# One landmark-attention and two-layer gated-MLP kernel: V of the second head group loaded ahead of the weights, landmark sums moved from VectorE to GpSimd

## The chip, the cores and the metric

The kernel runs on one core of a Trainium2 chip. The metric is device microseconds (us) of one execution. Before the change the median of three runs is 918.29 us (917.45 to 919.88).

## The reference, cut to what matters

Inputs: q, k, v of shape (4, 8, 576, 64): 4 batches, 8 heads, 576 tokens, head size 64; two gated layers with weights of 512 x 1536 (gate and value) and 1536 x 512 (out).

```python
q_lm = q.reshape(B, H, 32, 18, D).mean(axis=3)      # landmarks: means of 18 neighbouring tokens
k_lm = k.reshape(B, H, 32, 18, D).mean(axis=3)
A  = softmax(scale * q    @ k_lm.T)                 # 576 x 32
Bm = softmax(scale * q_lm @ k_lm.T)                 # 32 x 32
C  = softmax(scale * q_lm @ k.T)                    # 32 x 576
Z  = Bm.T / (norm1(Bm) * norminf(Bm) + 1e-6)
for _ in range(6): Z = 2 * Z - Z @ Bm @ Z           # an iterated inverse
attn = A @ Z @ C @ v                                # heads side by side: x of 2304 x 512
x = (silu(x @ w_gate) * (x @ w_val)) @ w_out
y = (sigmoid(x @ w2_gate) * (x @ w2_val)) @ w2_out
```

The landmark sums of q and k (18 tokens at a time) and the loading of v are what the change touches.

## The kernel before, in words

The eight heads of a batch are worked in two groups of four, so that four heads times 32 landmarks fill 128 partitions. One unit of attention work is (b, g): batch b, head group g; AORDER lists the eight units in order. q and k of a unit are loaded as 128 partitions (head, landmark) x 18 tokens x 64; v as 96 partitions.

`front(b, g)` does one unit. Its inner `lm_steps` runs first for k and then for q: the 18 tokens are summed to a tile `lm` of 64 elements (L121, VectorE), ScalarE copies it beside itself (L122), TensorE transposes it (L125, tile `lt`), ScalarE evicts it with a mask (L128, tiles `bdk`, `bdq`), and nine transposes (L135, `tp`) with three ScalarE copies (L136) lay out the tokens themselves in `kq`. Then come the scores of C (`cs`, L157 takes their maximum, L162 the exponential `e`), those of Bm (`bm`, `bs`), the transposes of e (`et`, `eT`), the product with v (`cv`, 48 matmuls), whose eviction L193 writes the second half of tile `bc`, and the scores of A (`as`, `sx`).

`back(b)` needs both units of a batch. L238 to L258 normalise Bm and work out the scale `rr`, a chain of small VectorE instructions; L273 to L284 are the six products of the iteration (`nw` on TensorE, 16 small matmuls, then `rw` on VectorE, each waiting for the other). The first `nw` reads `bc`, so it waits for `cv` of both groups. Iteration carries Z @ C @ v along, so its result `ut` is all that the first layer needs.

The first layer works on chunks c of 256 columns of d_ff: `uw_steps` (U) multiplies ut by the chunk's weights, `gv1_steps` (G) makes gate and value, `o1_steps` (O) the output. Weights are 32-bit words that two ScalarE and two VectorE instructions convert (L314, L317, L319, L323), out weights with one more each (L350, L351). They arrive in three `raw` buffers, so a load waits until ScalarE has read the buffer's former content.

The order is written out by hand as a list of words: `I0+F00 F01 B0+F10 U00 F11 J0 B1 G00 I1 F20 ...`, where F is a front, B a back, I and J finish weights, and "+" interleaves two. The framework's planner takes that order as priority and orders each engine's queue by what its own cost model says is ready; the engines then run their queues strictly in that order. All loads are issued by SyncE's queue, in order. Tiles of one tag share a fixed number of buffers: `in` (q and k) has 4, `vin` (v) 1, `lm` 2, `rw` 3, `wo` (out weights of a chunk, 8 KB a partition) 2.

Before the loop, k, q, v of unit (0,0) and k, q of (0,1) are loaded; v of (0,1) is asked for by `load_next` at the end of `cv` of (0,0), since `vin` has one buffer.

Of the kernel before, what the change touches and what calls it, by code (L numbers as in the profile page):

```python
# [5 lines left out]
F32 = mybir.dt.float32  # L6
# [3 lines left out]
ALU = mybir.AluOpType  # L10
AX = mybir.AxisListType
# [3 lines left out]
def nystrom_moe_kernel(tc, q, k, v, wg1, wv1, wo1, wg2, wv2, wo2, out):  # L15
    nc = tc.nc
    B, H, S, D = q.shape
    M = 32
    P = 128
    L = S // M  # L20
    R = 6
    TP = S // R
    HS = S // 2
    DM = H * D
# [7 lines left out]
    def pool(name, side=None, **kw):  # L32
        return tc.alloc_tile_pool(name=name, bufs=1, side=side, reuse_waits="tile", **kw)

    cst = pool("cst")
    per = pool("per")
    att = pool("att")
# [23 lines left out]
    def mm(o, l, r, start=True, stop=True):  # L61
        nc.tensor.matmul(o, l, r, start=start, stop=stop, skip_group_check=True)  # L62
# [3 lines left out]
    inq = {}  # L66

    def load_attn(b, which, g):
        if which == "v":
            t = att.tile([TP, 4, R, D], F32, tag="vin", name=f"vin{b}_{g}", bufs=1)  # L70
            nc.sync.dma_start(t, v[b, 4 * g:4 * g + 4].rearrange("h (p r) d -> p h r d", r=R))
        else:
            t = att.tile([P, L, D], F32, tag="in", name=f"{which}in{b}_{g}", bufs=4)
            src = {"q": q, "k": k}[which]
            nc.sync.dma_start(t, src[b, 4 * g:4 * g + 4].rearrange("h (t u) d -> (h t) u d", u=L))
        inq[which, b, g] = t

    NU = L // 2

    AORDER = [(b, g) for b in range(B) for g in range(2)]  # L80

    def flat(x):
        return x.rearrange("p a b -> p (a b)")

    def load_next(b, g, which):
        i = AORDER.index((b, g)) + (1 if which == "v" else 2)
        if i < len(AORDER):
            load_attn(AORDER[i][0], which, AORDER[i][1])

    def step(fill, n=1):  # L90
        while n and fill:
            try:
                next(fill[0])
                n -= 1
            except StopIteration:
                fill.pop(0)
# [4 lines left out]
    def small(tag, shape, nm_, bufs=2):  # L101
        return att.tile(shape, F32, tag=tag, name=f"{tag}{nm_}", bufs=bufs)

    def pst(b, shape, nm, g=0):

        tag = "n" if nm in ("nw", "ut") else "a"
        if b == 0:
            tag = {"tp": "gv", "cs": "o", "as": "o"}.get(nm, tag)
        return ptile(shape, tag, f"{nm}_{b}_{g}")

    def front(b, g):
# [3 lines left out]
        def sm(tag, shape, bufs=2):  # L115
            return small(tag, shape, nm_, bufs)

        def lm_steps(which):
            src = inq[which, b, g]
            lm = sm("lm", [P, 2, D])  # L120
            nc.vector.tensor_reduce(lm[:, 0], src.rearrange("p u d -> p d u"), axis=AX.X, op=ALU.add)  # L121
            nc.scalar.copy(lm[:, 1], lm[:, 0])  # L122
            yield
            ps = pst(b, [P, P], "lt", g)
            nc.tensor.transpose(ps, flat(lm), ident)  # L125
            bdt = sm("bd" + which, [P, 2, P], 1)
            for w in range(2):
                nc.scalar.activation(bdt[:, w], ps, AF.Copy, scale=pmask[:, w:w + 1])  # L128
            yield
            t = sm("kq", [P, NU, P])  # L130
            for i in range(3):
                ps = pst(b, [P, 3, P], "tp", g)
                for j in range(3):
                    u = 3 * i + j
                    nc.tensor.transpose(ps[:, j], flat(src[:, 2 * u:2 * u + 2]), ident)  # L135
                nc.scalar.copy(t[:, 3 * i:3 * i + 3], ps)  # L136
                yield
            load_next(b, g, which)
            return bdt, t
# [41 lines left out]
        for hf in range(2):  # L181
            ps = pst(b, [TP, 3, P], "et", g)
            for j in range(3):
                r = 3 * hf + j
# [14 lines left out]
        for i0, i1 in ((0, 5), (5, NU)):  # L199
            ps = pst(b, [P, 5, 2 * M], "as", g)  # L200
            for i in range(i0, i1):
                for h in range(4):
                    hs = slice(M * h, M * h + M)
                    mm(ps[hs, i - i0].rearrange("p (w m) -> p w m", w=2), qT[:, i, hs], bdk[:, :, hs])
            x = flat(ps[:, 0:i1 - i0]).rearrange("p (u m) -> p u m", m=M)
# [3 lines left out]
                                    op=ALU.subtract)  # L209
# [21 lines left out]
    def back(b):  # L231

        def sm(tag, shape, bufs=2):
            return small(tag, shape, b, bufs)

        bs, bsm, BC = BS[b]

        nc.vector.tensor_scalar(bsm, bsm, 1e-9, None, op0=ALU.add)  # L238
        nc.vector.reciprocal(bsm, bsm)
        nc.vector.tensor_tensor(bs, bs, bsm[:, :, None].to_broadcast([P, 2, M]), op=ALU.mult)  # L240
        nc.scalar.copy(BC[:, :, 0:M], bs)

        bmt = sm("bmt", [P, 2, M])
        nc.vector.transpose(out=flat(bmt), in_=flat(bs))
        nrm = sm("nrm", [P, 2, 2])
        nc.vector.tensor_reduce(nrm[:, 0], bs, axis=AX.X, op=ALU.add)
        nc.vector.tensor_reduce(nrm[:, 1], bmt, axis=AX.X, op=ALU.add)
        yield
        nb = sm("nb", [P, 4, M], 1)
        nc.vector.tensor_copy(nb, nrm.rearrange("p a b -> p (a b)")[:, :, None].to_broadcast([P, 4, M]))  # L250
        nbt = sm("nbt", [P, 4, M], 1)
        nc.vector.transpose(out=flat(nbt), in_=flat(nb))
        nmax = sm("nmax", [P, 2, 2])
        nc.vector.tensor_reduce(flat(nmax), nbt, axis=AX.X, op=ALU.max)
        rr = sm("rr", [P, 2])
        nc.vector.tensor_tensor(rr, nmax[:, 0], nmax[:, 1], op=ALU.mult)
        nc.vector.tensor_scalar(rr, rr, 1e-6, None, op0=ALU.add)
        nc.vector.reciprocal(rr, rr)  # L258
        yield


        def prod(x):
            ps = pst(b, [P, 2, 96], "nw")
            for g in range(2):
                for h in range(4):
                    hs = slice(M * h, M * h + M)
                    mm(ps[hs, g], x[hs, g, 0:M], x[hs, g])
            return ps

        ga = [a_steps(b, g) for g in range(2)]  # L270
        ps = prod(BC)
        RW = sm("rw", [P, 2, 96], 3)
        nc.vector.tensor_tensor(RW, ps, rr[:, :, None].to_broadcast([P, 2, 96]), op=ALU.mult)  # L273
        yield
        for it in range(5):
            ps = prod(RW)
            RW2 = sm("rw", [P, 2, 96], 3)
            nc.vector.scalar_tensor_tensor(RW2, RW, 2.0, ps, op0=ALU.mult, op1=ALU.subtract)
            RW = RW2
            step(ga)  # L280
            yield
        ps = prod(RW)
        UU = flat(sm("rw", [P, 2, 96], 3))[:, 0:P].rearrange("p (g d) -> p g d", g=2)
        nc.vector.scalar_tensor_tensor(UU, RW[:, :, M:], 2.0, ps[:, :, M:], op0=ALU.mult, op1=ALU.subtract)  # L284
        yield
        ps = pst(b, [P, P], "ut")
        nc.tensor.transpose(ps, flat(UU), ident)
        nc.vector.tensor_copy(flat(UT[b]), ps)
        yield
        while ga:  # L290
            step(ga)
            yield

    for g in range(2):
        for x in "kqv" if g == 0 else "kq":
            load_attn(0, x, g)


# [359 lines left out]
```

## Time and profile before

| what | value |
|---|---|
| median of three runs | 918.29 us |
| profiled execution | 917.74 us, of which the span from the first to the last instruction is 915.9 us |
| TensorE (PE) busy | 877.8 us, 96% |
| VectorE (DVE) busy | 542.2 us, 59% |
| ScalarE (ACT) busy | 391.7 us, 43% |
| GpSimd (POOL) busy | 0.7 us |

How to read the rows below. [...] A row of the timeline gives start, duration, engine, line, operation, the tiles written and read and how many instructions are merged; brackets at its end give how long the engine was idle before and what released it. A row of the groups by line gives busy us and mean ns behind the bar. A row for one tile gives durations in ns (minimum, median, maximum), then the first and last start. PE is TensorE's matmul, SPq is SyncE's queue, which issues the loads. All times are us from the start of the span.

### The profile page before, as it was taken

The page shows a single profiled execution, that of the slowest core. Times are in us where ns is not written, and L with a number is a line of the kernel's source. Part 1 is how long each engine was busy: PE and PEld are TensorE (multiplying, and loading weights), DVE is VectorE, ACT ScalarE, POOL GpSimd, SP SyncE. Part 2 cuts the span into 40 slices and gives each one's busy share as a digit, 9 for nine tenths or more (in the row PEclk, how much of TensorE's full clock was granted, in tenths as well). Part 3 has the DMA queues.
Part 4 walks back from the last instruction along what each step waited for, and adds up shares of the span by engine and source line. Part 5 has one row for each costly group of instructions (what it writes and reads, how often), then busy time and mean ns, then how long its engine had stood idle before and what let it go on. Part 6 is the DMA issues. An engine that isn't in the chain of part 4 may idle for free.

```text
span 915.9 us, 16047 instructions
## 1 busy us (share of the span) xinstructions
PE 877.8 (96%) x6588; PEld 741.9 (81%) x6588; DVE 542.2 (59%) x1093; ACT 391.7 (43%) x853; POOL 0.7 (0%) x6
## 2 busy tenths in 40 slices
PE   5499899999999999999999999999999999999997
PEld 4356877778898998998998888888888888888886
DVE  6988857746968678769961154346238236323343
ACT  5568568545725446428652263134116114111111
POOL 0000000000000000000000000000000000000000
PEclk9599999999999999999999999999999999999999
DMA  7666211003513113203110022003004000000132
GB/s 230 222 209 182 70 53 49 7 1 93 155 31 93 47 47 116 69 1 95 46 44 4 0 71 68 1 28 110 0 1 138 1 1 24 1 0 1 47 93 69
DMA packets 27081, 57.66 MB, mean 63 GB/s; under 512 B 4224, under 2 KB 7296, under 8 KB 27008
## 3 DMA queue, kind: packets, MB, share of 16 engines
q1 hardware_dynamic: 25280, 54.28, 19.6%
q10 hardware_dynamic: 1728, 2.36, 1.1%
q8 instruction: 51, 0.84, 0.4%
q14 instruction: 22, 0.18, 0.1%
HBM read 51.90 MB, written 4.72 MB: 62 GB/s over the span
## 4 chain that ended last, share of the span: by engine, by line
PE 88%; DVE 5%; ACT 4%; DMA 1%; issue 1%; SPq 0%; ACTq 0%
PE po L62 33%; PE pg L62 24%; PE pv L62 23%; PE pu L62 3%; PE tp L135 2%; PE nw L62 1%; DMA qin<-in_q_dram 1%; DVE lm L121 1%; PE cs L62 1%; ACT e L162 1%; PE as L62 1%; DVE hl L351 0%; ACT L162 0%; PE et L185 0%; DVE h L441 0%
## 5 line engine op out<-in xcount | busy, mean ns | idle before, releaser
L62 PE MATMUL po<-hh,wo 128*128 128x288 f32 x768 | 162.1, 302 | 1.1 <-DVE uw L351 0.7
L512 DVE TENSOR_TENSOR hf<-hf,pv 128x512 f32<-128x512 f32 (+1 forms) x60 | 38.0, 634 | 193.0 <-PE pv L62 193.0
L62 PE MATMUL po<-wo,h 128*128 128x512 f32 x648 | 152.2, 390 | 0.0
L62 PEld LDWEIGHTS po<-wo,h 128*128 128x128 f32 x648 | 121.1, 188 | 25.4 <-ACT h L350 0.3
L62 PEld LDWEIGHTS po<-hh,wo 128*128 128x128 f32 x768 | 123.0, 188 | 21.1 <-issue 14.4
L62 PE MATMUL pg<-AH,w 128*128 128x512 f32 (+1 forms) x480 | 136.1, 368 | 0.0
L62 PE MATMUL pv<-AH,w 128*128 128x512 f32 (+1 forms) x480 | 136.0, 368 | 0.0
L62 PE MATMUL po<-hl,wo 128*128 128x288 f32 x384 | 114.8, 299 | 0.3 <-DVE hl L351 0.3
L511 ACT ACTIVATE hf<-pg 128x512 f32<-128x512 f32 (+1 forms) x60 | 33.2, 554 | 165.4 <-PE pg L62 158.3
L62 PE MATMUL pg<-AH,uw 128*128 128x288 f32 x576 | 98.7, 298 | 2.3 <-ACT uw L350 1.8
L62 PEld LDWEIGHTS pg<-AH,w 128*128 128x128 f32 x480 | 87.3, 188 | 15.4
L62 PEld LDWEIGHTS pv<-AH,w 128*128 128x128 f32 x480 | 87.1, 189 | 15.0
L62 PE MATMUL pv<-AH,uw 128*128 128x288 f32 x576 | 96.7, 296 | 1.2 <-ACT sg L439 1.2
L62 PEld LDWEIGHTS pg<-AH,uw 128*128 128x128 f32 x576 | 83.1, 188 | 8.4 <-ACT uw L350 4.9
L350 ACT CAST h<-hf 128x512 fp32r<-128x512 f32 (+1 forms) x60 | 34.6, 576 | 123.2 <-DVE hf L512 123.2
L533 DVE TENSOR_TENSOR oacc<-po,oacc 128x512 f32<-128x512 f32 x90 | 61.9, 691 | 41.1 <-PE po L62 39.9
L62 PEld LDWEIGHTS pv<-AH,uw 128*128 128x128 f32 x576 | 82.9, 188 | 3.2 <-ACT sg L439 2.2
L62 PE MATMUL pg<-x1l,w 128*128 128x512 f32 x192 | 74.7, 389 | 0.0
L62 PE MATMUL pv<-x1l,w 128*128 128x512 f32 x192 | 74.7, 389 | 0.0
L62 PEld LDWEIGHTS po<-hl,wo 128*128 128x128 f32 x384 | 72.3, 188 | 2.4 <-issue 0.9
L467 DVE TENSOR_TENSOR acc<-po,acc 128x288 f32<-128x288 f32 x128 | 56.0, 452 | 18.2 <-PE po L62 17.5
L439 ACT ACTIVATE sg<-pg 128x288 f32<-128x288 f32 x96 | 39.2, 409 | 51.7 <-PE pg L62 51.1
(113 smaller groups left out, 1062.8 us busy)
## 6 DMA issues: line engine op xcount, KB each, us to landing
raw<-in_moe_w_out_dram SPq DMA_DIRECT2D x24, 512.0 KB, 4.2
raw<-in_moe_w_gate_dram SPq DMA_DIRECT2D x48, 128.0 KB, 3.3
raw<-in_moe_w_val_dram SPq DMA_DIRECT2D x48, 128.0 KB, 3.1
raw<-in_moe_w_gate_dram SPq DMA_DIRECT2D x24, 256.0 KB, 2.9
raw<-in_moe_w_val_dram SPq DMA_DIRECT2D x24, 256.0 KB, 3.3
kin<-in_k_dram SPq DMA_DIRECT2D x8, 576.0 KB, 3.9
qin<-in_q_dram SPq DMA_DIRECT2D x8, 576.0 KB, 5.7
vin<-in_v_dram SPq DMA_DIRECT2D x8, 576.0 KB, 4.9
```

Source lines behind the costliest of these rows:

```text
L62: nc.tensor.matmul(o, l, r, start=start, stop=stop, skip_group_check=True)
L121: nc.vector.tensor_reduce(lm[:, 0], src.rearrange("p u d -> p d u"), axis=AX.X, op=ALU.add)
L135: nc.tensor.transpose(ps[:, j], flat(src[:, 2 * u:2 * u + 2]), ident)
L162: nc.scalar.activation(e[:, :, w].rearrange("p r t j -> p j r t"), pcs[w].rearrange("p (j r) t -> p j r t", r=3), AF.Exp, bias=nmx, scale= ...
L350: nc.scalar.copy(hi, x)
L439: nc.scalar.activation(sg, pss[0], AF.Silu)
L467: nc.vector.tensor_tensor(sl, ps, sl, op=ALU.add)
L511: nc.scalar.activation(h, pss[0], AF.Sigmoid)
L512: nc.vector.tensor_tensor(h, h, pss[1], op=ALU.mult)
L533: nc.vector.tensor_tensor(acc, ps, acc, op=ALU.add)
```

## The change

v of (0,1) gets a buffer of tag `wo` and is loaded ahead of all weights; `load_next` looks one unit less far for later v. The landmark sum is made by six GpSimd additions as a tree (9x64, 4x64, 2x64, 64, and the last one twice, once into each half of `lm`) in place of one VectorE reduction and one ScalarE copy. Tag `lm` has one buffer in place of two, a new tag `ls` one, `rw` two in place of three.

```diff
     def load_attn(b, which, g):
         if which == "v":
-            t = att.tile([TP, 4, R, D], F32, tag="vin", name=f"vin{b}_{g}", bufs=1)
+            if (b, g) == (0, 1):
+
+                t = per.tile([P, 4 * DM], F32, tag="wo", name="vin0_1", bufs=2)
+                t = t[0:TP, 0:4 * R * D].rearrange("p (h r d) -> p h r d", h=4, r=R)
+            else:
+                t = att.tile([TP, 4, R, D], F32, tag="vin", name=f"vin{b}_{g}", bufs=1)
             nc.sync.dma_start(t, v[b, 4 * g:4 * g + 4].rearrange("h (p r) d -> p h r d", r=R))
...
     def load_next(b, g, which):
-        i = AORDER.index((b, g)) + (1 if which == "v" else 2)
-        if i < len(AORDER):
+        i = AORDER.index((b, g)) + 2
+        if which == "v" and i > 2:
+            i -= 1
+        if i < len(AORDER) and (which, *AORDER[i]) not in inq:
             load_attn(AORDER[i][0], which, AORDER[i][1])
...
-            lm = sm("lm", [P, 2, D])
-            nc.vector.tensor_reduce(lm[:, 0], src.rearrange("p u d -> p d u"), axis=AX.X, op=ALU.add)
-            nc.scalar.copy(lm[:, 1], lm[:, 0])
+            lm = sm("lm", [P, 2, D], 1)
+
+            x = sm("ls", [P, NU, D], 1)
+            nc.gpsimd.tensor_tensor(x, src[:, 0:NU], src[:, NU:], op=ALU.add)
+            nc.gpsimd.tensor_tensor(x[:, 0:4], x[:, 0:4], x[:, 4:8], op=ALU.add)
+            nc.gpsimd.tensor_tensor(x[:, 0:2], x[:, 0:2], x[:, 2:4], op=ALU.add)
+            nc.gpsimd.tensor_tensor(x[:, 0], x[:, 0], x[:, 8], op=ALU.add)
+            for w in range(2):
+                nc.gpsimd.tensor_tensor(lm[:, w], x[:, 0], x[:, 1], op=ALU.add)
             yield
...
-        RW = sm("rw", [P, 2, 96], 3)
+        RW = sm("rw", [P, 2, 96], 2)
...
-            RW2 = sm("rw", [P, 2, 96], 3)
+            RW2 = sm("rw", [P, 2, 96], 2)
...
-        UU = flat(sm("rw", [P, 2, 96], 3))[:, 0:P].rearrange("p (g d) -> p g d", g=2)
+        UU = flat(sm("rw", [P, 2, 96], 2))[:, 0:P].rearrange("p (g d) -> p g d", g=2)
...
     for g in range(2):
-        for x in "kqv" if g == 0 else "kq":
+        for x in "kqv":
             load_attn(0, x, g)
```

## Rows read from the trace of the kernel before

**Rows 1.** The page's busy time, span share and instructions of each engine.
```profile
PE 877.8 (96%) x6588; PEld 741.9 (81%) x6588; DVE 542.2 (59%) x1093; ACT 391.7 (43%) x853; POOL 0.7 (0%) x6
```
**Rows 2.** Stretches of the span.
```profile
24.00:30.00 6.00, 4.11 (x78) 3.09 (x78) 5.24 (x15) 5.22 (x14) 0.00 (x0) 0.53 0.91 319
30.00:44.00 14.00, 3.62 (x68) 2.56 (x69) 14.00 (x31) 6.87 (x15) 0.00 (x0) 0.50 0.66 197
44.00:60.00 16.00, 14.56 (x280) 8.09 (x279) 11.90 (x25) 7.71 (x21) 0.00 (x0) 0.87 0.52 152
60.00:120.00 60.00, 55.20 (x710) 42.78 (x704) 50.56 (x110) 42.66 (x103) 0.00 (x0) 1.00 0.45 135
```
**Rows 3.** The timeline of PE, where it stands still.
```profile
35.52 1.51 PE L62 MATMUL cv<-vin,eT 96*32 96x64 f32 x48 [3.46 <-DMA vin<-in_v_dram]
...
42.84 0.55 PE L62 MATMUL nw<-bc 32*32 32x96 f32 x8 [5.40 <-DVE bc L193]
```
**Rows 4.** The timeline of DVE from the second unit's end through batch 0's iteration.
```profile
26.34 0.14 DVE L239 RECIPROCAL bsm<-bsm 128x2 f32<-128x2 f32 x1
...
31.20 2.12 DVE L121 TENSOR_REDUCE lm<-kin 128x64 f32<-128x1152 f32 x1
...
34.26 2.08 DVE L121 TENSOR_REDUCE lm<-qin 128x64 f32<-128x1152 f32 x1
...
38.53 0.15 DVE L258 RECIPROCAL rr<-rr 128x2 f32<-128x2 f32 x1
...
42.52 0.27 DVE L193 TENSOR_SCALAR bc<-cv,rc 128x64 f32<-128x64 f32 x1
...
43.45 0.36 DVE L273 TENSOR_TENSOR rw<-nw,rr 128x192 f32<-128x192 f32 x1
...
54.16 0.29 DVE L284 SCALAR_TENSOR_TENSOR rw<-rw,nw 128x128 f32<-128x128 f32 x1 [0.65 <-PE nw L62]
```
**Rows 5.** The timeline of DVE, the same chain for batch 1.
```profile
77.28 0.17 DVE L238 TENSOR_SCALAR bsm<-bsm 128x2 f32<-128x2 f32 x1 [1.18 <-ACT bs L174]
...
82.81 0.14 DVE L258 RECIPROCAL rr<-rr 128x2 f32<-128x2 f32 x1
```
**Rows 6.** The timeline of SyncE's queue: the load of v of (0,1).
```profile
29.63 0.53 SPq L71 DMA_DIRECT2D vin<-in_v_dram  x1
```
**Rows 7.** The chain of waits at the start: q of (0,1), from issue to landing.
```profile
2.68 9.64 DMA qin<-in_q_dram
```
**Rows 8.** The instructions of tile lm.
```profile
L122 ACT COPY lm<-lm x16: 240/244/258, 6.7 to 148.9; 128x64 f32<-128x64 f32 x16
...
L121 DVE TENSOR_REDUCE lm<-kin x8: 2078/2141/2211, 4.6 to 142.3; 128x64 f32<-128x1152 f32 x8
```
**Rows 9.** Groups by line on POOL, whole span.
```profile
masks.py:199 POOL TENSOR_SCALAR_AFFINE_SELECT ident<-ident 128x128 f32<-128x128 f32 x1 | 0.3, 293 | 0.1
```
**Rows 10.** Groups by line on DVE, 30 to 44 us.
```profile
L220 DVE TENSOR_TENSOR sx<-sx,asm 128x576 f32<-128x576 f32 x1 | 0.7, 734 | 0.0
...
L240 DVE TENSOR_TENSOR bs<-bs,bsm 128x64 f32<-128x64 f32 x1 | 0.2, 215 | 0.0
```
**Rows 11.** The timelines of DVE, PE and ACT in the first unit, (0,0).
```profile
10.28 2.16 DVE L121 TENSOR_REDUCE lm<-kin 128x64 f32<-128x1152 f32 x1 [1.32 <-DMA kin<-in_k_dram]
...
11.54 1.18 PE L62 MATMUL cs<-kq,bdq 128*32 128x288 f32 x16
...
14.46 0.81 DVE L157 TENSOR_REDUCE cmx<-cs 128x1 f32<-128x288 f32 x2
...
15.84 0.68 ACT L162 ACTIVATE e<-cs,nmx 128x288 f32<-128x288 f32 x1
...
16.41 0.68 ACT L314 ACTIVATE cv<-raw 128x512 f32<-128x512 f32 x1
```
**Rows 12.** The timeline of PE, the second unit's landmark transposes, then a later stand.
```profile
20.46 0.47 PE L125 MATMUL lt<-ident,lm 128*128 128x128 f32 x2
...
99.20 0.65 PE L62 MATMUL as<-bdk,kq 128*32 128x64 f32 x32 [0.82 <-DVE bc L193]
```

## The prediction

> **What bounds the kernel now.** I read the page's busy shares first: TensorE is busy for 877.8 of the 915.9 us of span, GpSimd for 0.7 [rows 1]. So TensorE sets the time, and a change elsewhere pays only where TensorE stands still or runs at its low clock. A table of stretches shows where that is: from 24 to 30 us it is busy for 4.11 of 6 us, from 30 to 44 for 3.62 of 14, from 44 to 60 for 14.56 of 16, and then for 55.20 of 60 [rows 2]. [...] PE's timeline names the two waits: 3.46 us until v of (0,1) has landed, at 35.5, and 5.40 us until VectorE has written `bc`, at 42.8 [rows 3].
>
> The second is not the first's tail alone. The 48 `cv` matmuls are over at 37.0 (35.52 + 1.51), but their eviction starts at 42.52 [rows 3, 4]. VectorE's queue was ordered with late v in mind: ahead of it stand two landmark sums (2.12 and 2.08 us), batch 0's chain to `rr` (38.53), and parts of softmax and weight conversion. When `bc` comes, the iteration starts (first `rw` at 43.45, last at 54.16) [rows 4], and all of the first layer waits for that.
>
> The profiled execution took 917.74 us, 1.8 us more than its span and 0.55 us less than the median of 918.29. I work the sum out on 917.74 and add 0.55.
>
> **The change part by part.**
>
> *v of (0,1) moves ahead of the weights.* Its load was issued at 29.63 [rows 6], behind q of (0,1) by 27 us. Now it follows q directly. q of (0,1) landed at 12.3 (2.68 + 9.64) [rows 7], k of the same unit at 10.28 [rows 11], so one 576 KB load takes some 2.0 us in this stretch and v is there at about 14.4, well before it is wanted. The `cv` of (0,1) is then bound by `eT`, ready before 30, and `bc` is evicted near 30 in place of 42.52. On SyncE's queue one issue (0.53 us) is put ahead of all weights and taken away at 29.63, where v of (1,0) now takes its place; k and q of (1,1) stay behind it. The weights land up to 2.0 us later. What hides that: the first conversion ran at 16.41, when ScalarE got to it, with no wait in its row [rows 11], while the loads behind q had been landing since 12.3. If the cover is gone it costs at most those 2.0 us, once. I take 0. The `wo` buffer is free again after `cv`, before the second chunk's out weights want it: nothing.
>
> *What is late next.* With `bc` at 30, the first `rw` waits for `rr`. In the old queue the chain to `rr` took from 26.34 to 38.68, that is 12.3 us, in which VectorE had no pause. Two landmark sums in it go (4.2 us), which alone gives `rr` at 34.5. Batch 1's chain, in a busy queue without landmark sums in it, took 5.7 us (77.28 to 82.95) [rows 5]; I take that: `rr` at 26.3 + 5.7 = 32.0, first `rw` at 32.2 and not 43.45: 11.2 us earlier. Bounds: 8.9 (only the sums go) to 14 (rr at 29.3, half of batch 1's time). That is most of the 13.7 us that TensorE idles from 24 to 60 (36 less 22.3) [rows 2], so not all of it will show. VectorE's 25.9 us of work from 30 to 60, less four landmark sums of 2.1, is 17.5 us, now to be done in 30 less 11.2 = 18.8 us: 93% busy, and the `rw` stand in a queue. I take back 1.5 us for it (0 to 3).
>
> *The landmark sums on GpSimd.* Removed: 16 reductions of 2.14 us on VectorE, 34 us, and 16 copies of 0.244 us on ScalarE, 3.9 us [rows 8]. Added: 96 GpSimd additions. The trace has no two-input GpSimd instruction. One sum writes 576 + 256 + 128 + 3 x 64 = 1152 elements a partition. From below: on VectorE, 576 elements with two inputs took 734 ns and 64 took 215 [rows 10], on that line 0.73 + 0.41 + 0.28 + 3 x 0.215 = 2.1 us. From above: GpSimd's one-input select did 128 elements in 293 ns [rows 9], 2.29 ns each, so 2.6 us for 1152, and 5.3 us if two inputs are read one after the other. I take 3.2 us, near the one-input row with 0.1 us for each of the six steps, which wait for each other.
>
> [...]
>
> At the start GpSimd does k and q of (0,0) one after the other: 4.6 + 3.2 = 7.8 and 11.0. `cs` then starts near 12.3 (11.54 before) and ends near 13.5. But before, its maximum waited on VectorE until 14.46, behind the sums of (0,1), and the exponential started at 15.84 [rows 11]; now VectorE is free and it can start near 14.2, 1.6 us earlier. ScalarE has work queued there, so I count 0.5 us. The sums of (0,1) are done at 14.2 and 17.4, before TensorE asked for them at 20.46 [rows 12]. At 5.3 us a sum, the last would be ready at 4.6 + 4 x 5.3 = 25.8, which makes everything 5.3 us later than now and the first `rw` come at about 37.5. With one `lm` buffer, q's last additions wait for k's transpose; behind them only GpSimd's own queue waits: up to 0.6 us (the two additions and their hand-over, by L240's row), hidden behind the k transposes. `rw` with two buffers: each is read out before the one after the next is written: 0.
>
> *After 60 us* TensorE idles 4.8 us up to 120 [rows 2]; one stand of 0.82 us, at 99.20, is for a `bc` [rows 12] queued behind a landmark sum. I count 0.8.
>
> **Sum:** -11.2 + 1.5 - 0.5 - 0.8 = -11.0 us: 917.74 - 11.0 = 906.7, plus 0.55: **907.3 us**.
>
> **The rivals.**
>
> *GpSimd and VectorE get in each other's way* (about 911.3). From 30 on GpSimd would have four sums, 12.8 us, in the same 18.8 us in which VectorE is to do 17.5. If an instruction with two SBUF inputs, such as L220, can't run beside a GpSimd addition, and such are about half of VectorE's time there (my estimate), then 12.8/18.8 of 8.75 us, some 6 us, meet a busy GpSimd; about two thirds of that, 4 us, come on top: -7.0. For it: VectorE has no pause in this stretch. Against it: the old trace has no overlap to show either way. [...]
>
> *v is early and nothing else moves* (914.0). The planner may still put `bc` late: it stood 5.5 us behind a `cv` that was done. Then only the 3.46 us wait goes, and the 0.8: -4.3. Against it: the order was made for a late v.
>
> *More comes free* (902.9). `rr` at 29.3 (-14) with no backlog, and the six iterations, 10.7 us with landmark sums among them, shorten by one of these (2.1, less 1.0 that others take): with the 0.5 and 0.8, -15.4 or so. Against it: VectorE 93% busy.
>
> *Slower: GpSimd's chain becomes the bound* (923). TensorE's queue is strict; if the landmark transposes of (0,1) come late, all behind them does. The last of the first four sums comes at 4.6 + 4P, `bsm` 5.9 us later (20.46 to 26.34), `rr` 5.7 after that: the first `rw` falls on the old 43.45 at P = 6.8 us a sum. Beyond that the kernel is slower; at 8 us by 4.9: 917.74 + 4.9 + 0.55 = 923.2. For it: six dependent steps and a start for each. Against it: 6.8 is above my upper bound of 5.3.
>
> **How the numbers follow.** Chances: forecast 0.56 (its own range 903 to 911), interference 0.18, v alone 0.08, more 0.11, slower 0.07. The low end is the fourth case with the bound of the start's gain (1.6 and not 0.5) and of the stands after 60 (some 2 of the 4.8 us): 900. The high end holds the third case and a sum at 5.3 us (-11.2 + 5.3 + 1.5 - 0.8 = -5.2, 913.1), with up to 2.0 us for late weights: 916. Outside are the slow case and some 0.05 of the rest. A measurement of this kernel can't tell less than 0.3%, 2.75 us, from no change, that is 915.5 to 921.0. Faster: all but the slow case and 0.05: 0.88; same 0.05, from the third case with late weights and a P near 6; slower 0.07.
>
> **What would show it.** Right: no PE wait for `vin`; `bc` of (0,1) by 31 and the first `rw` by 34; TensorE busy for well over half of 30 to 44; VectorE's busy time down by some 34 us; GpSimd's up to about 50 us. Wrong: `lt` waiting for GpSimd for microseconds; L220 or L319 much longer than 0.7 us while GpSimd is busy; first `rw` after 38; or the iterations stretched well past 10.7 us.

## The result, and the profile after

The changed kernel takes **930.1 us** (median of 4 runs, 925.3 to 930.6) against 918.2 of the kernel before (4 runs): ratio 1.0115, 95% interval 1.0079 to 1.0151. It is slower by about 12 us; the prediction said 907.3, and its range ended at 916. The profiled execution is the fastest of the four, 925.3 us, 7.6 us above the 917.74 profiled before. The other three are some 5 us longer still, and part of the work below was to find out why.

The page's busy times, after:
```profile
PE 889.0 (96%) x6588; PEld 744.8 (81%) x6588; DVE 518.1 (56%) x1077; ACT 392.8 (43%) x839; POOL 64.0 (7%) x102
```
To be seen against [rows 1]: VectorE lost 24.1 us, not the 34.3 of its 16 reductions. Some 7 us of the 10.2 between are instructions that stayed and take longer now (their durations sum to 558.4 us before and 565.6 after); the rest is that neighbouring records overlap. And TensorE is busy for 11.2 us *more* with the same 6588 matmuls. With an equal count, either more of them ran at the low clock or fewer of them ran side by side; below both turn up.

The stretches of the span, after, which answer to [rows 2] (columns as there: start and end, length, busy time of PE, PEld, DVE, ACT and POOL with the number of instructions, then the granted TensorE clock, 1.00 being the full one, the busy share of the DMA engines, GB/s):
```profile
24.00:30.00 6.00, 3.71 (x146) 2.62 (x137) 5.59 (x20) 5.81 (x17) 1.06 (x1) 1.00 0.76 248
30.00:44.00 14.00, 7.65 (x81) 4.85 (x70) 13.87 (x28) 8.44 (x20) 10.81 (x14) 0.59 0.86 281
44.00:60.00 16.00, 14.11 (x253) 7.59 (x253) 11.54 (x29) 8.54 (x22) 9.24 (x13) 0.93 0.40 114
60.00:120.00 60.00, 55.41 (x641) 39.55 (x641) 39.25 (x96) 39.63 (x89) 16.56 (x26) 0.89 0.47 138
```
Up to 60 us things improved (TensorE is busy for 7.65 us of the stretch from 30 to 44, 3.62 before), though by less than half of what was forecast. But the stretch from 60 to 120, at 1.00 before, now has a granted clock of 0.89, and 641 matmuls were done in it where 710 had been. The time is lost there.

Where the lead went, from the timelines of the two profiled executions (us from the start of the span):

| | before | after | lead |
|---|---|---|---|
| first `rw` of batch 0 | 43.4 | 39.2 | 4.2 |
| first `pg` (first unit of the first layer) | 60.8 | 57.0 | 3.8 |
| `cv` of (1,1) | 77.7 | 73.9 | 3.8 |
| first `po` | 81.1 | 97.6 | -16.5 |
| last `pg` of G10 starts | 107.6 | 113.4 | -5.8 |
| first `pu` of U01 | 115.1 | 120.9 | -5.8 |
| 81st `pu`, and all from there to the end | 179.7 | 187.3 | -7.6 |

A lead of 3.8 us is there until 74 us and a lag of 5.8 at 115.

### The profile page after: what moved, and what is told of

Its sections match the earlier page's. It is cut to its first block, busy times and chain, and to the rows that moved or that the text cites. A ratio compares the mean times of both kernels' runs of the same rounds, so it can differ in the third digit from the quotient of the medians.

```text
span 923.5 us, 16153 instructions
## 1 busy us (share of the span) xinstructions
PE 889.0 (96%) x6588; PEld 744.8 (81%) x6588; DVE 518.1 (56%) x1077; ACT 392.8 (43%) x839; POOL 64.0 (7%) x102
## 4 chain that ended last, share of the span: by engine, by line
PE 90%; DVE 3%; ACT 3%; POOL 1%; DMA 1%; issue 1%; ACTq 0%; POOLq 0%; SPq 0%
PE po L62 33%; PE pg L62 24%; PE pv L62 23%; PE pu L62 4%; PE tp L148 2%; PE nw L62 1%; PE cs L62 1%; DMA qin<-in_q_dram 1%; PE cv L62 1%; PE as L62 1%; ACT e L175 0%; POOL ls L130 0%; PE et L198 0%; DVE hl L364 0%; DMA kin<-in_k_dram 0%
## 5 line engine op out<-in xcount | busy, mean ns | idle before, releaser
L62 PEld LDWEIGHTS pg<-AH,w 128*128 128x128 f32 x480 | 87.4, 189 | 15.4
```

## The experiments

After the first trace two theories stood: **Q**, SyncE's queue now has loads of k, q and v ahead of the second chunk's weights (behind the first four, nine more weight loads stood ahead of v of (1,1), now one), so those come late; and **G**, the sums on GpSimd hold up VectorE and the landmark transposes. The first four runs halve the change and mend the queue.

**The early v alone** (the hunks on `load_attn`, `load_next` and the first loads; the sums stay on VectorE):
```
-        for x in "kqv" if g == 0 else "kq":
+        for x in "kqv":
...
```


> Early v alone: v of (0,1) is loaded ahead of the weights as in the changed kernel, the landmark sums stay on VectorE, with the old numbers of buffers. Theory Q (queue): the loss comes from SyncE's queue, where early v moves the loads of batch 2's k and q and the load of v of (1,1) ahead of the second chunk's weights. Here 4 weight loads stand ahead of v of (1,1), in the changed kernel 1, in the old one 9. So part of the loss shows: 912 to 922 us, with the second chunk's weights late again. Theory G (GpSimd): the loss comes from the additions on GpSimd, which hold up VectorE and bring the landmark transposes late. Then it is gone here and the gain of early v is left: 907 to 914 us.

Measured: 929.99 us, 1.0126 (1.0110 to 1.0141). The early v by itself costs as much as both edits together, which is outside both ranges: more than Q allowed, and there is no sum on GpSimd in it.

**The sums on GpSimd alone** (the hunks on `lm`, `ls` and `rw`):
```
-            nc.vector.tensor_reduce(lm[:, 0], src.rearrange("p u d -> p d u"), axis=AX.X, op=ALU.add)
-            nc.scalar.copy(lm[:, 1], lm[:, 0])
+            nc.gpsimd.tensor_tensor(x, src[:, 0:NU], src[:, NU:], op=ALU.add)
...
```


> GpSimd sums alone: the landmark sums as in the changed kernel, with its numbers of buffers; v of (0,1) loaded where it was. Theory Q: SyncE's queue keeps the old order (9 weight loads ahead of v of (1,1)), so there is no large loss: 914 to 920 us. Theory G: the loss is here and without the gain of early v it is larger: 925 to 940 us.

Measured: 923.13 us, 1.0053 (1.0036 to 1.0070), again outside both ranges. Its DVE timeline (start, us, then line, operation, tiles, shapes, and in brackets the idle time before) shows where the sums' places in VectorE's queue went:
```profile
40.67 3.00 DVE L325 SCALAR_TENSOR_TENSOR cv<-cv,cv 128x512 uint32<-128x512 uint32 x2
...
46.62 0.28 DVE L199 TENSOR_SCALAR bc<-cv,rc 128x64 f32<-128x64 f32 x1
```
Conversions and softmax steps took them, two of the conversions at 1.5 us each (0.68 for the one at 45.25) beside GpSimd additions of 1.40 and 1.05 us (at 40.60 and 42.08), and `bc`, whose `cv` was over at 39.2, came at 46.62, later than the 42.52 of before [rows 4]. A freed place on an engine goes to whatever the planner puts there.

**The second chunk's weights ahead of v of (1,1) again**, otherwise the changed kernel:
```
+        if (b, g, which) == (1, 0, "v"):
+            load_to(9)
```


> The changed kernel with one edit: before v of (1,1) is asked for, the loads of the first nine weight pieces are put out, so that 8 loads of the second chunk's weights stand ahead of v of (1,1) in SyncE's queue, and not 1. Nothing of GpSimd's work changes. Theory Q: the lead of 3.8 us that the changed kernel has at the first pg (57.0 against 60.8 us) is kept: 911 to 917 us. Theory G: as the changed kernel, 922 us or more.

Measured: 924.58 us, 1.0072 (1.0052 to 1.0093).

**v of batches 1 to 3 issued from ScalarE's queue**, so that no weight load waits behind one:
```
-            nc.sync.dma_start(t, v[b, ...
+            (nc.sync if b == 0 else nc.scalar).dma_start(t, v[b, ...
```


> The changed kernel with v of batches 1 to 3 issued by ScalarE's queue and not by SyncE's, so that no wait for cv stands ahead of weight loads. Theory Q: 910 to 918 us. Theory G: as the changed kernel, 922 us or more. If ScalarE's own queue now stands behind cv, its instructions behind the issue are late, which shows as PE waiting for ACT.

Measured: 923.82 us, 1.0059 (1.0035 to 1.0082). Both win back half, less than Q asked for (911 to 917, and 910 to 918); as numbers they lie in G's range. An edit of the loads also changes what the planner does with the other queues, so neither theory is shown by them.

So I compared TensorE's queues. An iteration has seven products (`nw`), not the six of the words on the kernel before: one that reads `bc` and six that read `rw`. Between those of batch 1 stand, by kernel and gap (numbers are queue entries, and of a `pu`, `cs` or `bm` entry the trace shows two matmuls; the last two lines are experiments that follow):
```
before        po9 pg/pv11 tp6 lt1 | po4 tp4 lt1 | po1 tp5 | po1 tp3 cs4 | po3 cs4 | po8
after         pu2 tp9 lt2 | - | tp6 | pu1 tp3 cs5 | pu1 pg/pv3 cs3 | -
before, thin  pg/pv3 tp9 lt2 | po1 tp8 | tp1 cs1 | cs5 | po7 cs2 | po7
after, words  po12 pg/pv10 pu2 tp18 lt2 | cs5 | po4 cs3 | po7 | po1 pg/pv4 | pg/pv6 bm4
```
Before, 26 `po` and 11 `pg`/`pv` fill the gaps. After, there are three `pg`/`pv` and no `po`, since O00 has moved behind. That is theory **P**: the planner, by its own times, now runs batch 1's iteration ahead of the thick work of the first layer (long rows of `pg`, `pv` and `po`, 128x288 each), and TensorE goes through it with thin work alone (transposes, `cs`, the 32x96 products). The list of words that is given to the planner can change this with nothing else.

**P against Q and G, in the changed kernel**: B1 behind U10.
```
-        "I0+F00 F01 B0+F10 U00 F11 J0 B1 G00 I1 F20 U10 J1 O00 ...
+        "I0+F00 F01 B0+F10 U00 J0 F11 G00 I1 U10 B1 F20 J1 O00 ...
```


> The changed kernel, with batch 1's iteration (B1) moved behind U10 in the list of words that the planner is given (J0 F11 G00 I1 U10 B1 F20 J1 ... in place of F11 J0 B1 G00 I1 F20 U10 J1 ...); nothing is computed otherwise. In the queues that come of it only one weight load of the second chunk stands ahead of the load of v of batch 1's second head group, as in the changed kernel, but TensorE's queue has O00 and G10 matmuls between the seven products of batch 1's iteration, where the changed kernel has lt, tp and pu. Theory P (what costs the time is TensorE's order: an iteration with nothing thick beside it): U10 ends by 84 us, the first po comes by 88, the time is 914 to 920. Theory Q (the order of SyncE's queue makes the second chunk's weights late, whatever TensorE's order): pieces 8 to 10 are as late as in the changed kernel, TensorE waits for them now, 924 to 930. Theory G (GpSimd's additions hold up VectorE): 922 or more, since they are all there.

Measured: **916.02 us** (10 runs; before 918.04), 0.9982 (0.9964 to 1.0001). All 14 us are back, with every sum on GpSimd and one weight load ahead of v of (1,1). So the sums on GpSimd by themselves fall as the cause of the 12 us (G), and so does Q: the last gate and value weights of the second chunk landed at 71.3 us in the changed kernel and were converted at 88.7; here (second profile, a run of 917.3) they landed later, at 74.3, and were converted at 80.7.

**The same for the early v alone**, with F11 and B1 behind J0 and I1 (`... U00 J0 I1 F11 B1 G00 F20 U10 J1 ...`):

> The early v alone (sums on VectorE as before), with F11 and B1 moved behind J0 and I1 in the list of words. Two weight loads of the second chunk stand ahead of the load of v of batch 1's second head group (four without the new words, nine in the kernel before), and TensorE's queue has O00 and G10 matmuls between all products of batch 1's iteration. P: the 12 us of the early v alone go: 912 to 918, since the lead of its first iteration (first rw at 39 in place of 43 us) is kept. Q: loads stand worse than in the early v alone, so 928 or more.

Measured: 923.40 us, 1.0069 (1.0043 to 1.0094): 6.6 us better than the early v alone, with the loads in a worse order. Not what Q said, and not all that P said. P has a second difficulty here: the early v alone had 16 `po` between its products and lost as much as the changed kernel, which had none.

**The reverse, in the kernel before**: `... U00 F11 B1 J0 G00 F20 I1 U10 ...` makes the iteration thin.

> The kernel before, with B1 moved ahead of J0, and F20 ahead of I1, in the list of words: no early v, no sum on GpSimd. Eight weight loads stand ahead of v of batch 1's second head group (nine in the kernel before), but TensorE's queue has lt and tp in place of O00 between most products of batch 1's iteration, as the changed kernel has. P: slower than the kernel before by 3 to 8 us, 921 to 926, all of it lost between 80 and 115 us. Q: the queue of loads is the same but for one, so within 1.5 us of the kernel before. G: the same as the kernel before.

Measured: 922.61 us, 1.0055 (1.0036 to 1.0075). No edit of the change is in it, and the words cost 4.6 us. In the profile, which is of its slowest run (925.9; the other three took 922 to 923), the last `pg` of G10 starts at 113.9 us, about as in the changed kernel (113.4), not at 107.6.

**The control**: the words of the 916.02 in the kernel before.

> Control of the first run: the kernel before, with the words of that run (B1 behind U10). P: no loss, 914 to 919, as TensorE's queue has po and pg between the products already. Q: the order of loads is nearly that of before, 917 to 920.

Measured: 920.29 us, 1.0025 (1.0015 to 1.0036). The words are no gain by themselves: 2 us slower, just above P's range. Under these words the change is worth 4.3 us (920.29 to 916.02).

How does a thin queue cost time? From 80 to 96 us, the changed kernel, then the thin kernel before, then the changed kernel with the new words:
```profile
80.00:96.00 16.00, 15.13 (x122) 6.02 (x120) 8.58 (x18) 7.17 (x16) 7.03 (x10) 0.68 0.49 154
```
```profile
80.00:96.00 16.00, 15.10 (x227) 10.19 (x215) 11.67 (x32) 10.20 (x24) 0.00 (x0) 0.68 0.63 177
```
```profile
80.00:96.00 16.00, 14.30 (x254) 9.96 (x255) 15.79 (x39) 14.59 (x32) 9.64 (x12) 1.00 0.73 199
```
The granted clock drops to 0.50 within this stretch in the first two and stays at 1.00 in the third. In the changed kernel, PE and then DVE:
```profile
81.39 1.91 PE L62 MATMUL pu<-w,ut 64*32 64x512 f32 x2
83.24 0.47 PE L138 MATMUL lt<-ident,lm 128*128 128x128 f32 x1
83.64 1.91 PE L62 MATMUL pu<-w,ut 64*32 64x512 f32 x2
85.48 0.86 PE L62 MATMUL nw<-rw 32*32 32x96 f32 x16
```
```profile
86.41 0.35 DVE L291 SCALAR_TENSOR_TENSOR rw<-rw,nw 128x192 f32<-128x192 f32 x1 [3.53 <-PE nw L62]
```
Two `pu`, of a unit whose weights were converted just before, stand ahead of a product, at 1.91 us a pair where a pair takes 1.04 at full clock (91.31); VectorE waits 3.53 us for the product, so the next is late too.

Is it the clock (**C**) or the waits (**L**)? **Ballast**: four matmuls behind each product of batch 1, in the changed kernel.
```
+            if b == 1:
+                for _ in range(4):
+                    mm(pad[:, 192:480], AH[:, 0, 0:P], AH[:, 0, 0:HS])
```


> The changed kernel with four matmuls of 128x128 by 128x288 behind each of the seven products of batch 1's iteration. They read AH, write a part of the product's own PSUM tile that nobody reads, and so add nothing to the result: 28 x 0.3 us = 8.5 us of TensorE work that is pure ballast. TensorE's queue is otherwise the changed kernel's up to there, weights are as late as there. Theory C (what the thin iteration costs is TensorE's granted clock, 0.5 from 80.5 for 10.2 us): the stretch keeps 1.00 and the kernel loses nothing by the ballast, 922 to 928, or less than the changed kernel's 930.1 by 2 or more. Theory L (the thin iteration costs by its waits and its order, with the clock only a sign): the ballast comes on top, 930 to 938.

Measured: 926.02 us (923.94 to 929.48), 1.0070 (1.0045 to 1.0096). With some 8.5 us of useless work on TensorE (an estimate: 28 matmuls at the 0.30 us of a `pg` of the same size) the median is 4 us lower than without. The two intervals overlap, so this speaks for C without settling it; the clock from 80 to 96 is 0.93 in place of 0.68.

The profiles say more than the medians. From the first `pg` to the 81st `pu` the kernel before and the changed kernel run the same 1557 matmuls (columns as in [rows 2], before and then after):
```profile
60.79:179.66 118.87, 113.64 (x1557) 86.72 (x1557) 92.57 (x223) 85.14 (x203) 0.00 (x0) 1.00 0.30 87
```
```profile
57.04:187.30 130.26, 124.16 (x1558) 90.36 (x1558) 82.72 (x217) 88.83 (x199) 30.50 (x50) 0.95 0.31 88
```
The stretch is 11.4 us longer, of which 10.5 are busy time of TensorE and 0.9 are idle time. So waits are the small part, and the busy time has two sources. One is the low clock, 0.50: it lasts 13.7 us in this stretch (73.5 to 77.0 and 80.4 to 90.6), so it can make up at most half of that, 6.8, if nothing takes more than twice as long there (the pair of `pu` took 1.91 for 1.04 us). The other is that U10's 16 `pu` are pulled apart. Before, they stand in three runs:
```profile
65.17 1.04 PE L62 MATMUL pu<-w,ut 64*32 64x512 f32 x2
...
72.32 1.69 PE L62 MATMUL pu<-w,ut 64*32 64x512 f32 x8
...
74.59 1.05 PE L62 MATMUL pu<-w,ut 64*32 64x512 f32 x6
```
After, they stand in seven, the two slow pairs above and these five:
```profile
61.36 1.04 PE L62 MATMUL pu<-w,ut 64*32 64x512 f32 x2
...
69.07 1.05 PE L62 MATMUL pu<-w,ut 64*32 64x512 f32 x4
...
70.71 1.04 PE L62 MATMUL pu<-w,ut 64*32 64x512 f32 x2
...
91.31 1.04 PE L62 MATMUL pu<-w,ut 64*32 64x512 f32 x2
...
93.97 1.04 PE L62 MATMUL pu<-w,ut 64*32 64x512 f32 x2
```
At full clock the runs of 2, 4 and 6 took the same 1.04 to 1.05 us, and the seven runs took 9.0 us where three took 3.8. With the two slow pairs counted at 1.04, the pulling apart alone costs 3.5 us. The 6.8 and the 3.5 make 10.3 of the 10.5 us (an estimate, as 6.8 is a bound). The same stretch in other kernels, in us:

| | length | TensorE busy | idle | at the low clock | U10's `pu`: runs, us |
|---|---|---|---|---|---|
| before | 118.9 | 113.6 | 5.2 | 0 | 3, 3.8 |
| changed | 130.3 | 124.2 | 6.1 | 13.7 | 7, 9.0 |
| changed, ballast | 127.9 | 122.7 | 5.2 | 3.4 | 6, 6.3 |
| changed, words of the 916.02 | 120.1 | 115.5 | 4.6 | 0 | 4, 4.2 |
| early v alone | 129.9 | 122.5 | 7.4 | 10.2 | 4, 6.8 |
| before, thin | 125.9 | 119.5 | 6.4 | 10.2 | 3, 3.2 |

With 8.5 us of ballast in it the stretch is 2.3 us shorter than without. The thin kernel before has the low clock and no runs pulled apart, and loses 7.0; the new words take away both. No experiment changes only how U10's `pu` are grouped, so the split between the two sources is read from rows and is not tested by itself.

**One list of words, the four cases.** The early v alone with the words of the 916.02:

> The early v alone (sums on VectorE) with the words that made the changed kernel 916.0 (B1 behind U10). With it and the next run the four cases stand under one list of words: neither edit 920.3, both 916.0 are known. Theory P (order of TensorE's queue decides, sums matter little): 913 to 917. Theory G2 (the sums on GpSimd give a real gain of their own once the order is mended): 918 to 921 here.

Measured: 922.45 us, 1.0034 (1.0023 to 1.0045). The sums on GpSimd alone:

> The sums on GpSimd alone (v where it was) with the same words. The planner here puts O00 between nearly all products and two to three products less beside lt and tp. P: 917 to 921, since the first iteration starts late (first rw at 47 in place of 39 us) and nothing is won back. G2: 915 to 917.

Measured: 923.47 us, 1.0050 (1.0034 to 1.0066). Neither is 920.3, both 916.0: the numbers of P and of G2 fail in both runs, and the edits don't add up. The early v alone still has the low clock (0.79 from 48 to 64 us); the sums alone have a first `rw` at 48.2. So what a sum on GpSimd is worth by itself can't be read from any of these pairs.

**And v by ScalarE with these words:**

> Both edits, the same words, and v of batches 1 to 3 issued from ScalarE's queue, so that no load of weights stands behind a wait for v's buffer (seven of the second chunk's loads then stand behind k and q of batch 2 alone). P: weights as early as before and a filled iteration, 910 to 915, ahead of all others. If loads weren't what is left: within 2 us of the 916.0 of both edits with these words.

Measured: 926.28 us, 1.0080 (1.0064 to 1.0096), a clear miss. Its profile has the low clock from 48 to 64 (0.68) and from 76 to 96 (0.83). Which of its queues makes it so I did not find out.

**The same kernel twice.** The changed kernel and the one with the new words were profiled again, unedited, to see the runs that differ by 4 us.

> The changed kernel once more, nothing edited, to have a second profile of the same queues; the first was of a run of 925.3, three others took 930. C: if this run is at 929 to 931, its profile has one more stretch of granted clock 0.5 between 48 and 64 us (as the early v alone has at 52.5, 6.8 us long), and the loss appears there first; if it is at 925, the stretches are those of the first profile (32.7, 73.6, 80.5). L: the stretches are the same at either time, and the loss sits in a wait.

Measured: 929.15 us (before 918.84). PE from the last product of batch 0 to the first `pg`, in the first profile (925.3), then in this one:
```profile
50.90 1.04 PE L62 MATMUL pu<-w,ut 64*32 64x512 f32 x2
...
55.32 1.07 PE L62 MATMUL pu<-w,ut 64*32 64x512 f32 x10
...
57.04 0.40 PE L62 MATMUL pg<-AH,uw 128*128 128x288 f32 x1 [0.39 <-ACT uw L363]
```
```profile
51.98 1.18 PE L62 MATMUL pu<-w,ut 64*32 64x512 f32 x2
...
59.26 1.20 PE L62 MATMUL pu<-w,ut 64*32 64x512 f32 x10
...
61.12 0.40 PE L62 MATMUL pg<-AH,uw 128*128 128x288 f32 x1 [0.40 <-ACT uw L363]
```
The same instructions in the same order take 6.1 us in one and 9.1 in the other (first `pu` to first `pg`), and the wait at the end is the same 0.4. The granted clock from 48 to 64 is 1.00 and 0.79. First `pg` 4.1 us later (1.1 of it was there at the first `pu`, 3.0 come in this stretch), end of the span 3.9 us later: the difference is carried to the end.

> The changed kernel with B1 behind U10 once more, nothing edited; the first profile was of a run of 920.9, with a stretch of 0.5 from 50 to 61 us, eight others took 915.4 to 917.4. C: a run at 915 to 917 doesn't have that stretch, and its first pg is at 57 to 60 in place of 63.1. L: it has it as well.

Measured: 917.27 us; the first profile of this kernel was of a run of 920.91. From 48 to 64 us, this run and then the first:
```profile
48.00:64.00 16.00, 13.65 (x244) 8.05 (x236) 10.88 (x27) 8.10 (x20) 8.27 (x13) 0.97 0.48 132
```
```profile
48.00:64.00 16.00, 13.70 (x208) 6.60 (x201) 7.63 (x21) 4.47 (x13) 4.47 (x7) 0.68 0.34 98
```
First `pg` at 59.8 and 63.1, spans 915.5 and 919.1. So a low stretch costs time with nothing edited at all, as C says, twice. In these two pairs the same queues met the low clock in one run and not, or hardly, in the other (0.79 and 1.00, 0.68 and 0.97), at 3.9 and 3.6 us of span; what set it off, no row shows.

**Ballast in the first iteration**, in the kernel with the new words: two matmuls behind each product of batch 0 (`if b == 0: for _ in range(2): mm(pad[:, 192:320], ident, ident)`).

> The changed kernel with B1 behind U10, and two matmuls of ballast (128x128 by 128x128, the identity by itself, into a part of the product's PSUM tile that nobody reads) behind each of the seven products of batch 0's iteration; queues otherwise the same. C: the stretch of 0.5 at 50 to 61 us is gone or shorter in the profile, no run at 920 or more, median 913 to 916. L: 916 to 919, the ballast of 14 x 0.28 = 4 us partly on top.

Measured: 917.70 us (10 runs, 916.16 to 918.64; before 918.84), 0.9989 (0.9978 to 0.9999). The clock from 48 to 64 is 1.00, and no run is near 920, as C says; the median is no better, as L says: ballast pays for itself here and no more.

**Four of them:**

> The same with four matmuls of ballast per product (28 x 0.28 = 8 us). C: as with two, 913 to 917, unless the low clock before 48 us makes the ballast itself late (0.56 us each at half clock, 2.2 us a product where a product takes 1.8 us): then up to 919. L: 918 to 922.

Measured: 924.12 us, 1.0061 (1.0041 to 1.0080), above both theories' bounds. The iteration's last `rw` starts at 58.3 us in place of 52.0 with two: here the ballast is what the products wait for. (The 0.56 us was an estimate: a matmul of this size, the `lt` at 83.24 above, took 0.47 at the low clock.)

**Why `rr` came late.** In the changed kernel VectorE's queue holds weight conversions between the short instructions that make `rr`. I0 moved behind B0 takes them out: `F00 F01 B0+I0 F10 U00 J0 F11 G00 I1 U10 B1 F20 J1 ...`. (It also ends the interleaving of F10 with B0, and puts more loads of k, q and v ahead of the weights.)

> The changed kernel with B1 behind U10, and I0 (the first weights' loads and conversions) moved behind B0 as well: F00 F01 B0+I0 F10. In VectorE's queue no conversion then stands between bsm and rr, and the loads of the first weights come behind those of k, q and v of batch 1. Theory V (VectorE's queue kept rr late): first rw at 31 to 34 us (39.2 in the changed kernel). Theory G: the sums on GpSimd stretch the short instructions whatever stands between them, first rw at 37 or later. The time says little on this, since the first weights come late: with V the first pg is at 55 to 60 if they keep up, 912 to 917; at 62 or later if they don't, 919 to 926.

Measured: **913.48 us** (912.45 to 913.81; before 918.21), **0.9943 (0.9926 to 0.9959)**, the one version here that clearly beats both kernels. Its DVE timeline:
```profile
27.63 0.20 DVE L190 TENSOR_SCALAR rc<-csm 128x1 f32<-128x1 f32 x1
27.76 1.25 DVE L251 TENSOR_SCALAR bsm<-bsm 128x2 f32<-128x2 f32 x1
...
34.02 0.14 DVE L271 RECIPROCAL rr<-rr 128x2 f32<-128x2 f32 x1
34.23 0.89 DVE L332 SCALAR_TENSOR_TENSOR cv<-cv,cv 128x512 uint32<-128x512 uint32 x1
35.04 0.34 DVE L286 TENSOR_TENSOR rw<-nw,rr 128x192 f32<-128x192 f32 x1
```
First `rw` at 35.0, a microsecond past V's bound and two short of G's: V in the main. First `pg` is at 51.0 (57.0 in the changed kernel), the clock is 0.96 from 48 to 64 and 1.00 from 80 to 96, and TensorE is busy for 877.6 us, as before.

**The same words in the kernel before:**

> The same words in the kernel before: sums on VectorE, the second v not early in the list of instructions, though its load stands right behind k and q of batch 1 now, ahead of all weights but two. V: rr is done by 34 us, and the first rw waits for bc as far as v still comes late: 34 to 38 us. G: the same as V here, since GpSimd does nothing. The time: 915 to 924.

Measured: 923.72 us, 1.0054 (1.0039 to 1.0069). First `rw` at 35.6, as V says, and yet slower than before: the clock is 0.72 from 48 to 64, and the last `pg` of G10 starts at 114.6. An early iteration alone is worth nothing. Under these words the change is worth 10.2 us (923.72 to 913.48). That this is near the forecast's 11.0 is luck: the first `rw` comes only 0.6 us earlier.

## Why the prediction was wrong, point by point

*What held.* TensorE no longer waits for `vin`; `bc` of (0,1) was written at 31.02 ("near 30", "by 31"). A lead on the first `rw` does pass on to the first layer (4.2 us, of which 3.8 are there at the first `pg`). Neither the late weights nor the buffers were felt in this stretch: the first weights landed at 15.1 us in place of 12.7 (2.4 us later and not 2.0 at most), the first conversion started at 20.08 on ScalarE, 3.7 us later than before and with no wait in its row, and `pu` didn't wait for it.

*The first step that failed is "`rr` at 26.3 + 5.7 = 32.0, first `rw` at 32.2 and not 43.45: 11.2 us earlier".* It measured 4.2. The chain in VectorE's queue, conversions of weights included, first before (the end of `rr` is in [rows 4]):
```profile
26.08 0.15 DVE L238 TENSOR_SCALAR bsm<-bsm 128x2 f32<-128x2 f32 x1
...
27.15 0.69 DVE L319 SCALAR_TENSOR_TENSOR cv<-cv,cv 128x512 uint32<-128x512 uint32 x1
28.60 0.49 DVE L207 TENSOR_REDUCE amx<-as 128x10 f32<-128x320 f32 x1 [0.76 <-PE as L62]
29.00 0.68 DVE L323 SCALAR_TENSOR_TENSOR w<-cv,cv 128x512 uint32<-128x512 uint32 x1
...
37.92 0.68 DVE L319 SCALAR_TENSOR_TENSOR cv<-cv,cv 128x512 uint32<-128x512 uint32 x1
```
Then in the changed kernel:
```profile
26.59 0.16 DVE L251 TENSOR_SCALAR bsm<-bsm 128x2 f32<-128x2 f32 x1
...
28.56 0.69 DVE L332 SCALAR_TENSOR_TENSOR cv<-cv,cv 128x512 uint32<-128x512 uint32 x1 [0.19 <-ACT cv L330]
...
29.57 1.52 DVE L336 SCALAR_TENSOR_TENSOR w<-cv,cv 128x512 uint32<-128x512 uint32 x1
...
32.39 0.76 DVE L332 SCALAR_TENSOR_TENSOR cv<-cv,cv 128x512 uint32<-128x512 uint32 x1
...
33.34 0.82 DVE L336 SCALAR_TENSOR_TENSOR w<-cv,cv 128x512 uint32<-128x512 uint32 x1
...
35.83 1.12 DVE L269 TENSOR_TENSOR rr<-nmax 128x2 f32<-128x2 f32 x1
...
37.68 0.68 DVE L332 SCALAR_TENSOR_TENSOR cv<-cv,cv 128x512 uint32<-128x512 uint32 x1
38.28 0.15 DVE L271 RECIPROCAL rr<-rr 128x2 f32<-128x2 f32 x1
...
39.21 0.34 DVE L286 TENSOR_TENSOR rw<-nw,rr 128x192 f32<-128x192 f32 x1
```
From the first instruction on `bsm` to the end of `rr` it took 11.8 us (26.59 to 38.43), before 12.6 (26.08 to 38.68; the 12.3 of the prediction start at a later instruction than its 5.7 of batch 1). The two sums were gone, 4.2 us, but 3.6 came back. Five conversions make 4.5 us of the chain where three made 2.0; of these 2.4 us, 1.4 are two more conversions and 1.0 is that some took longer beside GpSimd (1.52, 0.82 and 0.76 us for 0.68). `rr` itself took 1.0 more, and small ones 0.2. The softmax steps take some 5 us in both. I had named VectorE's full queue and charged it 1.5 us, but after `rr`, not in it, and took batch 1's 5.7 us for the price. With the conversions moved away it was 6.4 (27.76 to 34.16), so the 5.7 was the right price of a chain that the planner didn't make.

*The step that turned the sign is "After 60 us ... I count 0.8".* It treated all that follows 60 us as fixed, and from 74 to 115 us the changed kernel loses 9.6 (a lead of 3.8 to a lag of 5.8). No rival had this: an earlier batch 1 pulls its iteration ahead of O00 and G10 in TensorE's strict queue, and the thin stretch runs at a granted clock of 0.50 for 10.2 us. That the order costs the time is shown both ways, by the words that put thick work back (916.0) and by those that take it away from the kernel before (922.6, 4.6 of the 12 us). What it costs by is in the profiles: at most 6.8 us of low clock, 3.5 us of `pu` runs pulled apart, 0.9 us of waits. The 1.8 us that are lost between 115 and 187 us, and why the planner comes to this order, were not looked into.

*The third is not in the sum at all:* the run's own clock. The profile of after was one without a low stretch between 48 and 64 us; the second profile has one and is 3.9 us longer. The three longer runs of the four (4.5 to 5.3 us) would fit that, but none of them was profiled.

*The sums on GpSimd.* All sixteen, by form (engine, operation, tiles and count, then shortest/median/longest ns):
```profile
L130 POOL TENSOR_TENSOR ls<-kin x8: 1399/1416/1612, 4.7 to 146.1; 128x576 f32<-128x576 f32 x8
L130 POOL TENSOR_TENSOR ls<-qin x8: 1399/1402/1411, 8.6 to 151.8; 128x576 f32<-128x576 f32 x8
L131 POOL TENSOR_TENSOR ls<-ls x16: 722/732/1186, 6.2 to 153.3; 128x256 f32<-128x256 f32 x16
L132 POOL TENSOR_TENSOR ls<-ls x16: 452/457/981, 7.0 to 154.1; 128x128 f32<-128x128 f32 x16
L133 POOL TENSOR_TENSOR ls<-ls x16: 317/319/718, 7.5 to 154.6; 128x64 f32<-128x64 f32 x16
L135 POOL TENSOR_TENSOR lm<-ls x32: 313/319/864, 7.9 to 170.0; 128x64 f32<-128x64 f32 x32
```
The medians sum to 1.42 + 0.73 + 0.46 + 0.32 + 2 x 0.32 = 3.6 us, 3.8 from first start to last end when alone (4.70 to 8.50) and 5.2 beside a busy VectorE (35.53 to 40.68): within the bounds of 2.1 and 5.3, above the 3.2 taken. The 0.1 us a step in the 3.2 was the author's estimate; alone, the gaps from one size to the next were 0.07 to 0.09. GpSimd's chain is not the bound (that rival wanted 6.8).

*The rival of interference* was real and smaller than the outcome: some 7 us on VectorE in all, of which 2.2 fall on the way to the first `rw`, most of it in two instructions: 0.84 (the conversion at 29.57, else 0.68 us) and 0.97 (`rr`, 0.146 us before). That it takes two SBUF inputs, as this rival supposed, no run shows: `bsm` in the fastest version has one and took 1.25 us (last section). It did not make the 12 us: the early v alone has none of it and is as slow (929.99). "v alone" (914.0) was 16 us off, since it counted only the wait that goes.

*Smaller things.* VectorE did pause in the old chain, for 0.76 us (at 28.60, above). "More comes free" adds up to -16.4 and not -15.4, that is 901.9. Of the signs, VectorE's busy time fell by 24.1 us and not by 34, GpSimd's rose to 64.0 and not 50, the first `rw` came after 38, and `lt` waited 1.95 us for GpSimd (at 33.66), though TensorE then stood for 3.2 us anyway until the first `rw`.

## What to carry to other kernels

A step that a planner schedules has no price of its own: what it frees is filled by other work, and what it brings forward pulls other work with it, so compare the queues of both kernels around the change before believing a saved wait. Where TensorE is the bound, look in the table of stretches for granted clock below 1.00 behind the change, and at TensorE's busy time with an equal count of matmuls: thin work ahead of thick work cost time here by the low clock (at most 6.8 us) and by matmuls pulled apart that had run side by side (3.5), and hardly by waits (0.9). And price a change under more than one order of the work: this one cost 12 us under the old list of words and gained 4 and 10 under two others. Before reading a difference of half a per cent from one profile, take a second one of the same kernel.

## What the runs showed of the hardware that was not expected

Two VectorE instructions of two elements a partition took 1.12 and 1.25 us beside GpSimd, where 0.15 and 0.16 were taken without (`rr` in the kernel before, `bsm` at 26.59 in the changed kernel). In the changed kernel `rr` (two inputs, 128x2) ran from 35.83 to 36.95, and this GpSimd addition from 35.53 to 36.93:
```profile
35.53 1.40 POOL L130 TENSOR_TENSOR ls<-qin 128x576 f32<-128x576 f32 x1 [1.92 <-DMA qin<-in_q_dram]
```
In the fastest version `bsm`, with one input tensor, ran from 27.76 to 29.01, and this one from 27.17 to 28.97:
```profile
27.17 1.80 POOL L130 TENSOR_TENSOR ls<-qin 128x576 f32<-128x576 f32 x1
```
Each ends with GpSimd's instruction to within 0.04 us, as if held until then. A one-element instruction (`rc`, 128x1, at 27.63) took 0.20 us beside the same addition, so not every short one is held; what makes the difference no row shows. In the two cases the wait is as long as the GpSimd instruction had still to run (1.10 and 1.21 us), so long GpSimd instructions were dear here beside short VectorE ones on a chain.

A low stretch of the clock in the middle of a kernel cost 3.9 and 3.6 us of span here (the two pairs above).

At full clock a run of `pu` took about the same time with 2 matmuls (1.04 us at 50.90) as with 10 (1.07 us at 55.32), but one of 8 took 1.69 (at 72.32 in the kernel before). So the planner that pulled such runs apart paid for nearly each part: U10's 16 took 3.8 us in three runs and, with the slow pairs counted at 1.04, 7.3 in seven.
